# One chunk store of batch 1 split into eight transfers of 6 partitions and one of 80, in an attention and token-update kernel

## The chip, the core and the metric

The kernel runs on one core of one Trainium2 chip. Its work is done by five engines with an instruction stream each: PE (matrix products and transposes), DVE (vector work and copies), ACT (activations and copies), POOL (which issues the loads, gathers and scatters here) and SP (which issues the stores). Transfers run on 16 DMA engines that all queues share. The metric is device time in microseconds (us) of one execution; less is better.

## The reference

For each of 4 batches of 6208 tokens by 256 channels, a channel-by-channel attention is computed, and then 128 chosen tokens of each batch get an update by a small two-layer network:

```python
qn = q / (np.linalg.norm(q, axis=1, keepdims=True) + 1e-06)
kn = k / (np.linalg.norm(k, axis=1, keepdims=True) + 1e-06)
s = kn.transpose(0, 2, 1) @ qn / tau
s = s - s.max(-1, keepdims=True)
a = np.exp(s)
a /= a.sum(-1, keepdims=True) + 1e-09
x = (v @ a).astype(np.float32)
...
scores = np.einsum('bsd,d->bs', x, w_gate)
out = x.copy()
for b in range(B):
    top_idx = np.argpartition(-scores[b], capacity)[:capacity]
    xe = x[b, top_idx]
    h = np.maximum(xe @ w1, 0.0)
    ye = h @ w2
    g = 1.0 / (1.0 + np.exp(-scores[b, top_idx]))
    out[b, top_idx] = x[b, top_idx] + g[:, None] * ye
```

## The kernel before

Each batch is cut into six chunks of 1024 tokens (eight tokens on each of 128 partitions) and a rest of 64 tokens. In the steps below, a batch b goes through these stages.

- **Loads.** POOL issues a load of 1024 tokens of q, of k or of v at L261, cast to bf16 on the way (`qk_ch`, `v_ch`; the rest is `qk_rem`, `v_rem`, L263). First come all q and k of a batch, then its v, then the next batch.
- **Products.** For each q and k chunk PE accumulates the 256 x 256 product and the norms (L426 and L430; for the last batch L411 and L441). When the last chunk is in, the softmax runs on DVE, ACT and PE (L453 to L544) and leaves `a_sb` and the score weights `aw_sb`.
- **v.** PE transposes each half chunk of v (L558), DVE or ACT copies it to `vt_sb` (L576, L579; for the last batch into freed `qk_ch` buffers), PE makes the scores (L607) and the outputs (L641), and ACT or DVE moves the outputs to a `stage` tile (L656, L659). `stage` has 9 buffers of one chunk.
- **Stores.** SP issues the store of a finished chunk: 1 MB, 8 KB from each of 128 partitions (L671), or 64 KB for the rest (L673). Stores of the last batch go as two halves.
- **The update.** Seven rounds of threshold search pick the 128 tokens (L683 to L797: DVE compares at L715, PE counts at L735). POOL then gathers their v rows (`vg`, L803), PE transposes them (L827) and runs the network (L837, L842, L868, L890), DVE makes `upd` (L894), and POOL scatters it over the stored rows (L908), behind the stores of that batch.

Batches are numbered 0 to 3; `L` is 3 and `E` is 2. The stores of batch 2, of batch 3 and of the last two chunks of batch 1 are held back until the last loads have landed: the first of them waits for a piece of the last v chunk, called `GATE`. The outputs of the last two chunks of batch 2 come last and get the update by two more products (L648).

The order of the instructions on every engine is fixed when the kernel is built, by a planner written into it. `Engines` keeps an estimated time for each engine, `Rings` an estimate of the DMA queues; at each step the main loop takes the piece of work that the estimates call ready, by priority. Nothing of this runs on the chip: there the engines run their fixed lists, and wait on semaphores. In `Rings`, `t` is the time up to which the queues are planned, and `lag` holds how far eight of the DMA engines are thought to be behind the others, since PE's instructions are themselves fetched by DMA: each fetch adds `FETCH` to one of the eight in turn, and a transfer is taken to land with the one furthest behind:

```python
self.lag[self.fetched % 8] += FETCH
...
self.lag = [max(0.0, x - (nxt - self.t)) for x in self.lag]
...
self.done[key] = self.t + tail + max(self.lag)
```

When PE would stand idle late in the kernel, the planner puts in products whose result nobody reads (`unread`, L593). Each DMA of SP raises one of eight semaphores in turn (DMAHW0 to DMAHW7 in the lists), and the DMA that takes a semaphore again waits until the transfer that used it last has landed; POOL's loads have eight of their own (DMASW0 to DMASW7).

## Time and profile before

| what | value |
|---|---|
| three timed executions | 258.79, 260.25, 260.44 us (median 260.25) |
| the profiled execution | 259.43 us |
| its span, first to last instruction | 257.4 us |
| PE, DVE, ACT, POOL busy | 206.8, 104.3, 99.4, 56.2 us |
| HBM read and written | 78.91 and 25.95 MB |

The profiled execution took 2.0 us more than its span; the span is what the rows below divide. "Share" of the DMA engines is the mean busy share of all 16, and it can pass 1 a little since a packet's time overlaps the next one's. GB/s counts the bytes on the SBUF side, so a casting load of 1 MB from HBM counts half.

### The profile page before, as it was taken

To read this page: it belongs to the slowest core of one execution; us is meant where nothing else is said; L and a number is where in the kernel's file an instruction comes from. 1 tells how busy PE (TensorE), PEld (TensorE's weight loads), DVE (VectorE), ACT (ScalarE), POOL (GpSimd) and SP (SyncE) were. 2 spreads that over 40 slices of the span, in tenths; PEclk is the share of its full clock that TensorE was granted. 3 is DMA by queue.
4 is the path that set the end of the run, shared out by engine and by line. 5 is a ranking of instruction groups with operands and counts; after the bars stand their busy time and mean duration, and the time that the engine had idled before them with its cause. 6 is when DMAs were issued, how large, how long until landed. Compare 5 with 4: busy or idle time off the path is not lost.

```text
span 257.4 us, 6080 instructions
## 1 busy us (share of the span) xinstructions
PE 206.8 (80%) x2585; PEld 171.4 (67%) x2585; DVE 104.3 (41%) x414; ACT 99.4 (39%) x182; POOL 56.2 (22%) x105
## 2 busy tenths in 40 slices
PE   0099697788888969999998759689998989887980
PEld 0068476676767849997676549577776879665860
DVE  0200002657552263436660011656657266676230
ACT  2800003630000587763943001660233298364750
POOL 8223223123204230100034123213214200001301
PEclk9999889799999997999999799999999999999998
DMA  6999999999999999999999999999999997999995
GB/s 236 259 218 213 213 213 211 215 212 213 213 214 212 214 259 288 279 333 313 315 291 333 308 221 211 214 212 214 211 215 212 212 211 185 402 425 414 401 419 233
DMA packets 16844, 66.84 MB, mean 260 GB/s; under 512 B 2097, under 2 KB 3634, under 8 KB 13618
## 3 DMA queue, kind: packets, MB, share of 16 engines
q0 software_dynamic: 12528, 38.93, 75.8%
q1 hardware_dynamic: 4290, 27.53, 26.4%
q8 instruction: 20, 0.33, 0.5%
q14 instruction: 6, 0.05, 0.0%
HBM read 78.91 MB, written 25.95 MB: 407 GB/s over the span
## 4 chain that ended last, share of the span: by engine, by line
DMA 54%; PE 24%; issue 8%; ACT 4%; DVE 4%; POOL 2%; POOLq 1%; SPq 0%; ACTq 0%
DMA qk_ch<-in_k_dram 29%; DMA qk_ch<-in_q_dram 13%; DMA v_ch<-in_v_dram 12%; PE o_ps L641 8%; PE s_ps L426 4%; PE g_ps L430 4%; ACT stage L659 2%; PE vt_ps L558 2%; PE m_ps L735 1%; PE sc_ps L607 1%; POOL qk_ch L261 1%; ACT vt_sb L576 1%; DVE qk_ch L579 1%; DVE cmp L715 1%; PE g_ps L641 1%
## 5 line engine op out<-in xcount | busy, mean ns | idle before, releaser
L426 PE MATMUL s_ps<-qk_ch 128*128 128x256 bf16 x288 | 68.8, 284 | 21.4 <-DMA qk_ch<-in_k_dram 21.4
L430 PE MATMUL g_ps<-qk_ch 128*128 128x256 bf16 x288 | 68.6, 284 | 0.0
L659 ACT COPY stage<-o_ps 128x512 f32<-128x512 f32 x79 | 44.7, 590 | 40.0 <-PE o_ps L641 38.0
L426 PEld LDWEIGHTS <-qk_ch 128*128 128x128 bf16 x288 | 29.3, 102 | 28.3 <-DMA qk_ch<-in_k_dram 23.3
L641 PE MATMUL o_ps<-a_sb,vt_sb 128*128 128x256 bf16 (+1 forms) x278 | 40.2, 274 | 3.1 <-ACT stage L659 2.1
L641 PEld LDWEIGHTS <-vt_sb 128*128 128x128 bf16 (+1 forms) x294 | 27.5, 98 | 9.9 <-issue 6.0
L430 PEld LDWEIGHTS <-qk_ch 128*128 128x128 bf16 x288 | 29.3, 102 | 4.5
L558 PEld LDWEIGHTS <-v_ch 128*128 128x128 bf16 x384 | 24.5, 101 | 4.2 <-issue 3.5
L558 PE MATMUL vt_ps<-ident_b,v_ch 128*128 128x128 bf16 x328 | 24.9, 226 | 2.9 <-ACT vt_sb L576 2.9
L261 POOL DMA_DIRECT2D qk_ch<-in_q_dram x25 | 13.8, 552 | 44.4 <-PE vt_ps L558 8.7
L261 POOL DMA_DIRECT2D v_ch<-in_v_dram x25 | 13.5, 551 | 29.3 <-DMA qk_ch<-in_q_dram 18.2
L466 DVE SCALAR_TENSOR_TENSOR junk<-g_ps,ident_f 128x128 f32<-128x128 f32 x6 | 1.7, 292 | 44.6 <-ACT e L457 44.5
L261 POOL DMA_DIRECT2D qk_ch<-in_k_dram x25 | 13.6, 545 | 26.7 <-DMA v_ch<-in_v_dram 15.3
L739 DVE TENSOR_REDUCE cnt<-m_ps 128x8 f32<-128x392 f32 (+2 forms) x28 | 12.0, 429 | 16.3 <-PE m_ps L735 15.9
L579 DVE COPY vt_sb<-vt_ps 128x1024 bf16<-128x1024 bf16 x20 | 13.5, 689 | 12.0 <-PE vt_ps L558 12.0
L715 DVE SCALAR_TENSOR_TENSOR cmp<-sc,wl,tab 128x392 bf16<-128x392 f32 x28 | 17.5, 627 | 1.0
L908 POOL DMA_INDIRECT out_dram<-upd,idx x4 | 4.0, 991 | 62.8 <-DMA out_dram<-stage 31.3
L576 ACT COPY vt_sb<-vt_ps 128x1024 bf16<-128x1024 bf16 (+1 forms) x19 | 16.3, 906 | 1.2 <-PE vt_ps L558 1.0
L457 ACT COPY e<-g_ps 128x256 f32<-128x256 f32 x3 | 1.1, 372 | 31.5 <-PE g_ps L430 31.5
L607 PE MATMUL sc_ps<-aw_sb,vt_sb 128*128 128x2 bf16 (+1 forms) x294 | 11.1, 164 | 1.5 <-DVE sc L683 0.6
L441 PE MATMUL s_ps<-qk_ch 128*128 128x256 bf16 x96 | 11.9, 273 | 0.0
L607 PEld LDWEIGHTS <-vt_sb 128*128 128x128 bf16 (+1 forms) x294 | 10.1, 96 | 2.7 <-DVE vt_sb L579 1.6
(180 smaller groups left out, 268.7 us busy)
## 6 DMA issues: line engine op xcount, KB each, us to landing
out_dram<-stage SPq DMA_DIRECT2D x18, 1024.0 KB, 14.3
qk_ch<-in_q_dram POOLq DMA_DIRECT2D x23, 512.0 KB, 14.6
qk_ch<-in_k_dram POOLq DMA_DIRECT2D x23, 512.0 KB, 18.9
v_ch<-in_v_dram POOLq DMA_DIRECT2D x23, 512.0 KB, 16.9
out_dram<-stage SPq DMA_DIRECT2D x12, 512.0 KB, 8.2
stage<-in_moe_w_dram SPq DMA_DIRECT2D x2, 1024.0 KB, 5.0
qk_ch<-in_q_dram POOLq DMA_DIRECT2D x2, 256.0 KB, 16.0
qk_ch<-in_k_dram POOLq DMA_DIRECT2D x2, 256.0 KB
```

The source lines that it names most:

```text
L261: ins = nc.gpsimd.dma_start(out=t[:, rows, :], in_=lview(src, b, d)[:, rows, :])
L426: nc.tensor.matmul(s_ps[:, cc, :].rearrange("p (i c) -> p i c", i=2), lhsT=pair[:parts, 1, s, cc * P:(cc + 1) * P], rhs=pair[:parts, :, s, ...
L430: nc.tensor.matmul(g_ps[:, cc, :].rearrange("p (i c) -> p i c", i=2), lhsT=blocks[:parts, at, :], rhs=blocks[:parts, at:at + step + 1:step ...
L441: nc.tensor.matmul(s_ps[:, cc, :], lhsT=kt[:parts, s, cc * P:(cc + 1) * P], rhs=qt[:parts, s, :], start=d == FIRST and s == 0 and cc == 0, ...
L558: nc.tensor.transpose(vt_ps[:, cc, j, :parts], in_=vt[:parts, v0 + j, cc * P:(cc + 1) * P], identity=ident_b[:parts, :parts])
L576: nc.scalar.copy(vt_sb[:, :, :n, :parts], vt_ps[:, :, :n, :parts])
L579: nc.vector.tensor_copy(vt_sb[:, :, :n, :parts], vt_ps[:, :, :n, :parts])
L607: nc.tensor.matmul(sc_ps[:parts, col, :], lhsT=vt_sb[:, cc, j, :parts], rhs=aw_sb[:, cc, :], start=cc == 0 and col == 0, stop=cc == 1 and ...
L641: nc.tensor.matmul(o_ps[:parts, pj, :], lhsT=vt_sb[:, cc, j, :parts], rhs=a_sb[:, cc, :], start=pj == 0 and cc == 0, stop=last and cc == 1 ...
L659: nc.scalar.copy(st[:parts, rows, :], o_ps[:parts, :m, :])
L715: nc.vector.scalar_tensor_tensor(out=cmp, in0=sc[:, :, None].to_broadcast([P, NCOL, NTHR]), scalar=wl[:, i, NTHR:NTHR + 1], in1=tab[:, Non ...
L739: nc.vector.tensor_reduce(out=cnt9[:, 0:NTHR], in_=mps[:, 0:wide * NTHR].rearrange("p (s j) -> p j s", s=wide), axis=AX.X, op=ALU.add)
```

## The change

The first chunk store of batch 1 is issued in nine DMAs where there was one. Eight of them take 6 partitions each, four partitions apart, out of the first 48 (partitions 0, 4, ..., 20; then 1, 5, ..., 21; and so on, and the same from 24 on); the ninth takes partitions 48 to 127. The planner gets a kind of transfer (`few`) that moves `t` on and takes its duration off all eight entries of `lag`; these may now be below zero and then stay so, and a landing adds no less than zero. As landings are estimated anew, the planner also writes a different order from batch 1 on.

```diff
--- before.py
+++ after.py
@@ -40,8 +40,8 @@
         self.lag[self.fetched % 8] += FETCH
         self.fetched += 1
 
-    def add(self, ring, ready, dur, key, tail):
-        self.q[ring].append((ready, dur, key, tail))
+    def add(self, ring, ready, dur, key, tail, few=False):
+        self.q[ring].append((ready, dur, key, tail, few))
 
     def run(self, until):
         while True:
@@ -51,14 +51,16 @@
             nxt = max(self.t, min(self.q[r][0][0] for r in heads))
             if nxt > until:
                 return
-            self.lag = [max(0.0, x - (nxt - self.t)) for x in self.lag]
+            self.lag = [max(min(0.0, x), x - (nxt - self.t)) for x in self.lag]
             self.t = nxt
             able = [r for r in heads if self.q[r][0][0] <= nxt]
             r = able[0] if len(able) == 1 else 1 - self.last
-            ready, dur, key, tail = self.q[r].pop(0)
+            ready, dur, key, tail, few = self.q[r].pop(0)
             self.last = r
             self.t = nxt + dur
-            self.done[key] = self.t + tail + max(self.lag)
+            if few:
+                self.lag = [x - dur for x in self.lag]
+            self.done[key] = self.t + tail + (0.0 if few else max(0.0, max(self.lag)))
 
     def landing(self, key):
         if key in self.done:
@@ -201,6 +203,8 @@
     LATE = order[-2:]
     BACK = order[-2:]
     LROWS = len(LATE) * RPP
+    UNEVEN = (1, order[0])
+    SIXES = 48
 
     def groups(ci):
         return [(ci, 0, 4), (ci, 4, 4)] if ci < NFULL else [(ci, 0, 1)]
@@ -998,11 +1002,26 @@
         if late(b, ci):
             dep = max(dep, rings.landing(("scatter", E)))
         parts = (2 if b == L else 1) if ci < NFULL else 1
+        uneven = (b, ci) == UNEVEN
+        if uneven:
+            st = stage_of[(b, ci)]
+            for i, p0 in enumerate(range(0, SIXES, 24)):
+                for j in range(4):
+                    ps = slice(p0 + j, p0 + j + 21, 4)
+                    nc.sync.dma_start(out=view(out, b, ci)[ps], in_=st[ps])
+                    issued = eng.issue("sp", 0.75, dep)
+                    key = ("st", b, ci, i, j)
+                    rings.add(1, issued + 0.65, 0.32, key, 0.45, True)
+                    stored[b].append(key)
         for h in range(parts):
             key = ("st", b, ci) if h == parts - 1 else ("st", b, ci, h)
             issued = eng.issue("sp", 0.42, dep)
-            rings.add(1, issued + 0.65, STORE / parts + 0.009 if ci < NFULL else 0.2, key, 0.45)
-            ins = emit_store(b, ci, h, parts)
+            share = (P - SIXES) / P if uneven else 1.0
+            rings.add(1, issued + 0.65, STORE * share / parts + 0.009 if ci < NFULL else 0.2, key, 0.45)
+            if uneven:
+                ins = nc.sync.dma_start(out=view(out, b, ci)[SIXES:P], in_=st[SIXES:P])
+            else:
+                ins = emit_store(b, ci, h, parts)
         stored[b].append(key)
         if not late(b, ci):
             held[b] -= 1
```

On SP, at the stores around the change: before, chunks 4 and 5 of batch 0, chunk 0 of batch 1, its rest, and its chunks 1 to 3 (`128x2048` is a chunk, `64x256` the rest; in brackets what a DMA waits for).

```order
L671 DMA out_dram<-stage 128x2048 [waits DMAHW0_49,Activation_49]
L671 DMA out_dram<-stage 128x2048 [waits DMAHW1_49,Activation_49]
L671 DMA out_dram<-stage 128x2048 [waits DMAHW2_49,Activation_49]
L673 DMA out_dram<-stage_rem 64x256 [waits DMAHW3_49,Activation_49]
L671 DMA out_dram<-stage 128x2048 [waits DMAHW4_49,Activation_49]
L671 DMA out_dram<-stage 128x2048 [waits DMAHW5_49,Activation_49]
L671 DMA out_dram<-stage 128x2048 [waits DMAHW6_49,Activation_49]
```

The same place now, from chunk 5 of batch 0 to chunk 1 of batch 1:

```order
L675 DMA out_dram<-stage 128x2048 [waits DMAHW1_49,Activation_49]
L1011 DMA out_dram<-stage 6x2048 [waits DMAHW2_49,Activation_49]
L1011 DMA out_dram<-stage 6x2048 [waits DMAHW3_49]
L1011 DMA out_dram<-stage 6x2048 [waits DMAHW4_49]
L1011 DMA out_dram<-stage 6x2048 [waits DMAHW5_49]
L1011 DMA out_dram<-stage 6x2048 [waits DMAHW6_49]
L1011 DMA out_dram<-stage 6x2048 [waits DMAHW7_49]
L1011 DMA out_dram<-stage 6x2048 [waits DMAHW0_49]
L1011 DMA out_dram<-stage 6x2048 [waits DMAHW1_49]
L1022 DMA out_dram<-stage 80x2048 [waits DMAHW2_49]
L677 DMA out_dram<-stage_rem 64x256 [waits DMAHW3_49,Activation_49]
L675 DMA out_dram<-stage 128x2048 [waits DMAHW4_49,Activation_49]
```

The short transfers go once round the eight semaphores, so the seventh and the eighth of them now wait for the landing of chunks 4 and 5 of batch 0, and the rest and chunks 1 to 3 of batch 1 stand behind them.

On PE, where the gathered rows (`vg`) of batch 1 are transposed: before, this stands between products of batch 2's q and k.

```order
L430 LDWEIGHTS qk_ch
L430 MATMUL g_ps<-qk_ch 128x256
L827 LDWEIGHTS vg [waits DMASW0_49]
L827 MATMUL vt_ps<-ident_b,vg 128x128
...
L426 LDWEIGHTS qk_ch [waits DMASW7_49]
L426 MATMUL s_ps<-qk_ch 128x256 [waits DMASW6_49]
```

Now it stands behind all of those products, behind the softmax of batch 2 and behind its first transposes of v:

```order
L562 LDWEIGHTS v_ch
L562 MATMUL vt_ps<-ident_b,v_ch 128x128
L831 LDWEIGHTS vg [waits DMASW2_49]
L831 MATMUL vt_ps<-ident_b,vg 128x128 [waits Activation_49]
...
L611 LDWEIGHTS vt_sb
L611 MATMUL sc_ps<-aw_sb,vt_sb 128x2 [waits DVE_49]
```

The whole update of batch 1 has moved with it by some 200 instructions of PE's list. That list has 18 unread products less than before (36 rows of 5136).

On PE near the end, where the gathered rows of batch 3 are transposed: before, behind the last output products (L641, L648).

```order
L648 LDWEIGHTS late_oh
L648 MATMUL o_ps<-d_b,late_oh 128x256
L827 LDWEIGHTS vg [waits DMASW4_49]
L827 MATMUL vt_ps<-ident_b,vg 128x128
...
L593 LDWEIGHTS ident_b
L593 MATMUL sc_ps<-w_sb,ident_b 128x256
L837 LDWEIGHTS a_sb
L837 MATMUL m_ps<-vgt,a_sb 128x128 [waits DVE_49]
```

Now two output tokens' worth of products, eight in all, stand between this transpose and the products that need its copy:

```order
L831 LDWEIGHTS vg [waits DMASW4_49]
L831 MATMUL vt_ps<-ident_b,vg 128x128
...
L645 LDWEIGHTS vt_sb
L645 MATMUL o_ps<-a_sb,vt_sb 128x256 [waits Activation_49]
...
L841 LDWEIGHTS a_sb
L841 MATMUL m_ps<-vgt,a_sb 128x128 [waits DVE_49]
```

So the transpose is issued eight products earlier, and the unread product that stood in the gap is gone.

## Rows read from the trace of the kernel before

**Rows 1.** The profile's page: DMA busy tenths in 40 slices; the chain's shares by engine.

```profile
DMA  6999999999999999999999999999999997999995
...
DMA 54%; PE 24%; issue 8%; ACT 4%; DVE 4%; POOL 2%; POOLq 1%; SPq 0%; ACTq 0%
```

**Rows 2.** Stretches: length, busy of each engine, clock, DMA share, GB/s.

```profile
core 0: us, PE busy (x) PEld busy (x) DVE busy (x) ACT busy (x) POOL busy (x), PEclk, DMA share, GB/s
...
140.00:145.00 5.00, 2.00 (x13) 1.28 (x11) 0.00 (x0) 0.00 (x0) 0.86 (x2) 0.79 1.03 328
...
200.00:210.00 10.00, 9.09 (x149) 7.58 (x142) 3.80 (x21) 4.90 (x11) 1.58 (x3) 1.00 1.09 213
```

**Rows 3.** The same view in short stretches, where the loads end.

```profile
214.00:214.50 0.50, 0.50 (x19) 0.48 (x17) 0.00 (x0) 0.50 (x3) 0.00 (x0) 1.00 0.81 164
214.50:216.00 1.50, 1.34 (x26) 1.04 (x23) 0.32 (x2) 1.08 (x4) 0.00 (x0) 1.00 0.59 108
216.00:216.50 0.50, 0.50 (x16) 0.50 (x14) 0.30 (x1) 0.00 (x0) 0.00 (x0) 1.00 0.35 62
216.50:217.00 0.50, 0.50 (x13) 0.50 (x11) 0.50 (x2) 0.16 (x1) 0.00 (x0) 1.00 0.06 12
```

**Rows 4.** The page's DMA queues: packets, MB, share of 16 engines.

```profile
q8 instruction: 20, 0.33, 0.5%
```

**Rows 5.** The same view as Rows 2, in the stretch of the held stores.

```profile
218.00:222.00 4.00, 3.40 (x76) 2.94 (x74) 2.36 (x5) 0.77 (x1) 0.00 (x0) 1.00 1.01 389
222.00:226.00 4.00, 3.93 (x41) 2.85 (x38) 3.02 (x14) 2.97 (x6) 0.00 (x0) 1.00 1.01 424
...
222.00:248.00 26.00, 23.27 (x247) 18.63 (x244) 12.92 (x53) 16.78 (x31) 2.98 (x3) 1.00 1.02 414
...
252.00:253.00 1.00, 0.00 (x0) 0.00 (x0) 0.00 (x0) 0.00 (x0) 0.83 (x1) 1.00 1.08 459
...
255.00:256.00 1.00, 0.00 (x0) 0.00 (x0) 0.00 (x0) 0.00 (x0) 0.00 (x0) 0.75 0.08 33
```

**Rows 6.** SP: its wait for the gate (us, times, longest), and the first held store.

```profile
SPq L671 <- DMA v_ch<-in_v_dram: 87.5, 1, 87.5
...
216.69 0.33 SPq L671 DMA_DIRECT2D out_dram<-stage  x1
```

**Rows 7.** The end, timeline of DVE and POOL: start us, us, what, and idle before it.

```profile
251.06 0.48 DVE L894 SCALAR_TENSOR_TENSOR upd<-o_ps,gate,xe 128x256 f32<-128x256 f32 x1 [0.45 <-PE o_ps L890]
...
251.86 0.97 POOL L908 DMA_INDIRECT out_dram<-upd,idx  x1 [7.91 <-DVE upd L894]
```

**Rows 8.** SP's timeline around the changed store; last, the page's median time to landing.

```profile
110.68 3.37 SPq L671 DMA_DIRECT2D out_dram<-stage  x2
...
120.03 0.33 SPq L671 DMA_DIRECT2D out_dram<-stage  x1
120.45 0.48 SPq L673 DMA_DIRECT2D out_dram<-stage_rem  x1
123.71 5.41 SPq L671 DMA_DIRECT2D out_dram<-stage  x3
...
out_dram<-stage SPq DMA_DIRECT2D x18, 1024.0 KB, 14.3
```

**Rows 9.** Timeline of POOL, then of PE, in batch 2's first part.

```profile
110.70 0.53 POOL L261 DMA_DIRECT2D qk_ch<-in_k_dram  x1 [2.76 <-DMA qk_ch<-in_k_dram]
131.00 1.01 POOL L908 DMA_INDIRECT out_dram<-upd,idx  x1 [19.77 <-DVE cnt L739]
...
143.48 0.39 PE L426 MATMUL s_ps<-qk_ch 128*128 128x256 bf16 x1 [3.00 <-DMA qk_ch<-in_k_dram]
151.55 0.29 PE L827 MATMUL vt_ps<-ident_b,vg 128*128 128x128 bf16 x2 [3.06 <-DMA vg<-in_v_dram,idx]
```

**Rows 10.** PE's timeline: unread products, the last transpose of v, batch 3's gathered rows.

```profile
210.86 1.04 PE L593 MATMUL sc_ps<-w_sb,ident_b 128*128 128x256 bf16 x8
...
220.36 0.61 PE L558 MATMUL vt_ps<-ident_b,v_ch 128*128 128x128 bf16 x8
...
247.00 0.28 PE L827 MATMUL vt_ps<-ident_b,vg 128*128 128x128 bf16 x2
```

## The prediction

> **What bounds the kernel now.** I read the page's slices first. The 16 DMA engines show 9 tenths or more in all slices but the first, one near 215 us and the last, and the chain that ended last is DMA for 54% [rows 1]. Then I asked each stage what ends last there. Where loads run alone the DMA share is 1.09 at 213 GB/s [rows 2]; that is all 16 engines at work. From 222 to 248 us, where the held stores run, it is 1.02 at 414 GB/s, still 1.08 at 252, and 0.08 only at 255 [rows 5]. So the kernel is a queue of transfers with one hole in it: SP sits on the gate for 87.5 us and issues the first held store at 216.69, when the first piece of the last v chunk has landed [rows 6].
>
> The hole is what this change is about. At 214 us the share begins to fall: 0.81, then 0.59 for 1.5 us, 0.35, 0.06 [rows 3]. Against 1.09, a share of 0.59 is 0.54 of 16, some 8.7 engines. So about seven engines have done all their loads by 214.2 us, and about nine go on to some 216.3, the last to 216.6. A transfer has landed when its slowest engine has, so the whole tail waits for those nine. They lag by 2.3 us. The work left after 214.0 is 0.5 x 0.81 + 1.5 x 0.59 + 0.5 x 0.35 + 0.5 x 0.06 = 1.50 us of share; spread evenly at 1.09 it ends at 214.0 + 1.37 = 215.4. Perfect balance is therefore worth 1.2 us at most.
>
> A cause fits in size: 20 instruction fetches took 0.5% of 16 engines' span [rows 4], 0.005 x 16 x 257.4 / 20 = 1.0 us each. 17 or so of them before the gate, on eight engines alone, make 2.1 us each. No view of this trace names the engine of a packet, so that it is eight fixed ones is inferred.
>
> **The change, part by part.** *The split store.* Held stores move 424 GB/s [rows 5], so 1 MB (1.049 million bytes) takes 2.47 us, and one of the eight rows of 8 KB that each engine then has takes 0.309 us. The changed store gives 80 partitions evenly, 5 rows an engine, and 48 in sixes. The trace holds no transfer of 6 partitions. Its bounds are six engines with one row each time, 8 rows extra, or fewer engines, for instance three with 16 extra; I take six, since the planner's 0.32 us per transfer is nearest to the one row of 0.309. Six engines then carry 13 rows where they had 8, +1.55 us; the other ten carry 5, -0.93 us. If the six are among the seven that are early, they finish at 214.2 + 1.55 = 215.75, and the laggards at 216.6 - 0.93 = 215.7. Both meet: the gate comes 0.9 us earlier. The store stands at 120 us [rows 8], and the DMA share never falls from there to 214 [rows 1], so nothing evens the offset out on the way.
>
> The rule that settles which engines is one of the Trainium skill, DMA: Bandwidth & Descriptors, section "Why a DMA increments its semaphore by 16 and not by 1": a transfer from SP uses the largest number of engines up to 16 that divides its slowest dimension, and the lowest-numbered ones. By that a transfer of 6 partitions runs on engines 0 to 5 and one of 80 on all 16; no run here shows it.
>
> *SP's queue.* Nine DMAs of some 0.3 to 0.5 us [rows 8] in place of one are not the price. The seventh and eighth short ones wait for the semaphores of the chunks issued at 110.68 and by 114.05, and a store takes 14.3 us to land [rows 8]: they go at about 125 and 128, the 80 partitions behind them at 128.5, and the rest and chunks 1 to 3 of batch 1 follow in a row. Before, these went at 120.45, 123.71 and up to 129.1 [rows 8], so chunk 1 comes some 6 us later and chunk 3 about 2. Who waits for that? POOL's scatter of batch 1 stands behind the held stores, 100 us on; `stage` has nine buffers, and chunk 1's is needed again in batch 2. What hides it is the load queue: POOL issued a load at 110.70 and no more until 131.00, and PE still waited for a k load at 143.48 [rows 9], with the DMA share at 1.03 between 140 and 145 [rows 2]. So loads fill the engines while stores are late, and the same bytes end at the same time. If that cover were gone, the engines would idle some 2 to 6 us. I put it at nothing.
>
> *The order.* The update of batch 1 moves behind batch 2's softmax. PE's wait of 3.06 us for its gather [rows 9] goes from that place; late there next are the q and k loads themselves, which PE then meets without that delay. 18 unread products go, at 1.04 / 8 = 0.13 us each [rows 10] 2.3 us of PE. PE needs some of that: the last transpose of v stands at 220.36 [rows 10], 3.8 us after the last load, so PE and the copies, not the load, hold the selection there, and an earlier gate alone would not move it. With up to 5 us of PE time released and loads that land 0.9 earlier, I take PE to follow by at least 0.9; that is the softest step.
>
> *The end.* The last scatter goes at 251.86, released by `upd`, which ends at 251.54 [rows 7], while the DMA engines work through stores until after 253 [rows 5]. Both chains start from the gate or from PE and come 0.9 earlier. The gathered rows of batch 3 are now transposed eight products (8 x 0.11 = 0.9 us) earlier than 247.00 [rows 10]; that can give the update up to 0.5 us, or nothing if the gather has just landed by then. More than that is not to be had, since the stores must drain.
>
> **Sum.** Gate -0.9; SP 0; order 0 beyond keeping pace; end 0 to -0.5, taken as 0. The profiled execution took 259.43, 2.0 more than its span: 259.43 - 0.9 = 258.5. The median of the three runs is 260.25, and the four executions together average 259.7; I forecast 259.7 - 0.9 = 258.8.
>
> **The rivals.** *A, slower: the short transfers cost more than their bytes.* Six engines have no slack left after +1.55, so what each transfer costs beyond 0.309 us goes into the gate eight times; from 0.9 / 8 = 0.11 us each the gain is gone. The nearest row is the stretch 218 to 222, which has a store of 64 KB among its chunks and moves 389 GB/s in place of 424: 4 x 35 / 424 = 0.33 us lost at most to it [rows 5]. Eight times 0.33 is 2.6, the gate comes 1.7 later, 261.4. Fewer than six engines is the same mechanism: three have 21 rows, 13 x 0.309 = 4.0 more, end at 218.2, and give 261.3; two have 29, 6.5 more, end at 220.7, and give 263.8. Against it: the share in that stretch is 1.01, so the engines did not stand still.
>
> Here the Trainium skill speaks against the change: the same page, Rules for kernel authors, has many small transfers put into one, as under 64 KB one pays mostly overhead; its anatomy of one DMA gives some 2 us fixed for each on POOL's path. If the engines were held for all of it, eight would be 16 us, an estimate from that page, and the kernel near 274. The rows above bound what an engine is held at 0.33.
>
> *B, no gain: the six are the laggards, or a mix.* Then the nine end at 216.6 + 1.55, and the time is 259.7 + 1.5 = 261.2; with a mix it lies between that and no change. The trace speaks neither way on which engines lag.
>
> *C, PE does not follow.* The gate moves, but selection and update keep their times, and the scatter goes at 251.86 as before: 259.7. If the products of q and k that now stand among batch 1's threshold rounds wait for loads, it is 1 to 2 us worse, 261.
>
> *D, more.* PE runs free by 3 us and the update's chain was the last thing: 256.9 at best, as stores still drain until 252.
>
> **How the numbers follow.** The forecast has 0.52 (its own range 257.8 to 259.8), C 0.18, A 0.10, B 0.10, D 0.10. About 1%, 2.6 us, is what a measurement of this kernel can tell from no change. Faster by over 1% needs D's far end: 0.06. Slower by over 1% needs A with two engines, or a dearer transfer, or C gone wrong by 3 us: 0.07. The rest, 0.87, lies within 1%. The range reaches from D's 256.9 to B's and A's 261.4, and leaves out A's far end.
>
> **What would show it.** In the changed trace, the share after the loads' end should fall from 1.09 to near nothing within about 1 us instead of 2.5, and the first held store should be issued near 215.8. SP should show waits of some 5 and 3 us among the short transfers, and the DMA share should stay at 1.03 or more between 120 and 150. PE should have no wait of 3 us for the gather of batch 1, and the last transpose of v should come by 219.5. I am wrong if the share still falls in two steps, or if the gate comes earlier and the last scatter does not.

## The result and the profile after

The changed kernel took 262.88 us (median of four runs, 262.22 to 263.55) where the kernel before took 259.93 beside it (258.79 to 260.44). The ratio is 1.011, with a 95% interval from 1.0076 to 1.0144: some 3 us slower, and outside the range of the forecast. In this and all later ratios, runs over 1.5% above their kernel's fastest are left out: one of f1 and four of g1 (the profiled one among them in both), one of g3, one of f2, and one of the kernel before beside the experiments (683.74 us). The profiled execution took 263.55 us, the longest of the four, with a span of 262.0, 4.6 more than the span before.

The page of the changed kernel first: the granted clock and the DMA busy tenths in 40 slices, and the chain that ended last.

```profile
PEclk9999999977999999999997699669999997999999
DMA  7999999999999999999999999999999997599995
...
PE 46%; DMA 27%; ACT 9%; DVE 7%; issue 7%; POOL 1%; POOLq 1%; ACTq 0%; DVEq 0%
```

Two things differ from [rows 1]. Near the loads' end stands a 7 as before, but a 5 follows it: the held stores run, and then stop once more. And the chain has turned round: DMA was 54% of it and PE 24%; now PE is 46% and DMA 27%. Next the stretches that answer to [rows 2, 3, 5] (columns as there).

```profile
140.00:145.00 5.00, 2.26 (x11) 1.65 (x12) 0.00 (x0) 0.00 (x0) 1.44 (x3) 0.64 1.05 324
...
165.00:175.00 10.00, 9.04 (x87) 7.06 (x87) 4.42 (x19) 5.64 (x13) 2.13 (x4) 0.52 1.07 212
...
214.00:215.00 1.00, 1.00 (x17) 0.94 (x15) 0.49 (x2) 1.00 (x3) 0.00 (x0) 1.00 1.14 215
215.00:216.00 1.00, 1.00 (x12) 0.90 (x11) 0.51 (x3) 1.00 (x5) 0.00 (x0) 1.00 0.84 154
216.00:217.00 1.00, 0.52 (x9) 0.34 (x7) 0.90 (x6) 1.00 (x2) 0.00 (x0) 1.00 0.21 39
217.00:218.00 1.00, 0.60 (x12) 0.48 (x13) 0.97 (x5) 1.00 (x3) 0.00 (x0) 1.00 0.15 29
...
226.00:230.00 4.00, 3.90 (x59) 3.07 (x58) 2.49 (x9) 1.66 (x3) 0.00 (x0) 1.00 0.21 84
```

The loads end in two steps again, and the second is now long and thin: 0.21, then 0.15 of the engines, two or three of 16, where nine of them ended [rows 3]. From 226 to 230 us, in the middle of the held stores, the share is 0.21, where [rows 5] have 1.02 from 222 to 248 us. From 165 to 175 us PE's granted clock is 0.52, that is 1.2 GHz for nearly all of it. SP's timeline, around the changed store and at the gate (answers to [rows 6, 8]):

```profile
118.81 7.97 SPq L1011 DMA_DIRECT2D out_dram<-stage  x8
126.83 0.44 SPq L1022 DMA_DIRECT2D out_dram<-stage  x1
127.38 0.52 SPq L677 DMA_DIRECT2D out_dram<-stage_rem  x1
...
217.39 0.33 SPq L675 DMA_DIRECT2D out_dram<-stage  x1
```

The gate opens at 217.39, 0.7 later than before and not 0.9 earlier. PE's timeline shows where it waited and what ran behind the waits:

```profile
142.74 0.40 PE L430 MATMUL s_ps<-qk_ch 128*128 128x256 bf16 x1 [4.56 <-DMA qk_ch<-in_k_dram]
...
152.99 0.28 PE L430 MATMUL s_ps<-qk_ch 128*128 128x256 bf16 x1 [1.67 <-DMA qk_ch<-in_k_dram]
...
157.90 0.28 PE L430 MATMUL s_ps<-qk_ch 128*128 128x256 bf16 x1 [1.25 <-DMA qk_ch<-in_k_dram]
...
165.78 1.19 PE L517 MATMUL m_ps<-diag,ones_f 128*128 128x256 f32 x2 [3.10 <-DVE diag L505]
...
172.04 1.86 PE L872 MATMUL o_ps<-xet,w_sb 128*128 128x128 bf16 x16
```

The 3-us wait for batch 1's gather [rows 9] is gone, as the order said. PE now meets three waits for k, where it had one of 3.00, and one of 3.10 inside batch 2's softmax; the update of batch 1 follows (L872: its network) at half clock. From there PE stays late. On DVE the last scores of batch 3 are reduced from 228.39, and the last `upd` [rows 7] comes 5.6 later than before:

```profile
228.39 0.15 DVE L688 TENSOR_REDUCE sc<-sc_ps 64x1 f32<-64x2 f32 x1 [0.44 <-PE sc_ps L611]
...
256.70 0.48 DVE L898 SCALAR_TENSOR_TENSOR upd<-o_ps,gate,xe 128x256 f32<-128x256 f32 x1 [0.45 <-PE o_ps L894]
```

The first of these rows stood at 222.15 in the kernel before (DVE's timeline):

```profile
222.15 0.15 DVE L684 TENSOR_REDUCE sc<-sc_ps 64x1 f32<-64x2 f32 x1 [0.44 <-PE sc_ps L607]
```

The hole from 226 to 230 us is PE's lateness too. Among SP's waits from 218 to 232 us the longest, which ends at 228.7, is for the copy of an output chunk that isn't made yet:

```profile
SPq L675 <- ACT stage L663: 8.3, 1, 8.3
```

### The profile page after: what moved, and what is told of

It reads as the page before. It is cut to its first block, busy times and chain, and to the rows that moved or that the text cites. A ratio compares the mean times of both kernels' runs of the same rounds, so it can differ in the third digit from the quotient of the medians.

```text
span 262.0 us, 6054 instructions
## 1 busy us (share of the span) xinstructions
PE 212.5 (81%) x2567; PEld 173.7 (66%) x2567; DVE 106.7 (41%) x417; ACT 96.3 (37%) x179; POOL 56.4 (22%) x105
## 4 chain that ended last, share of the span: by engine, by line
PE 46%; DMA 27%; ACT 9%; DVE 7%; issue 7%; POOL 1%; POOLq 1%; ACTq 0%; DVEq 0%
DMA qk_ch<-in_k_dram 27%; PE o_ps L645 8%; PE s_ps L430 6%; PE g_ps L434 6%; PE vt_ps L562 5%; PE sc_ps L611 4%; PE s_ps L445 4%; ACT stage L663 4%; PE g_ps L415 3%; ACT vt_sb L580 3%; PE m_ps L739 2%; PE o_ps L894 2%; PE o_ps L872 1%; ACT e L526 1%; POOL qk_ch L265 1%
## 5 line engine op out<-in xcount | busy, mean ns | idle before, releaser
L430 PE MATMUL s_ps<-qk_ch 128*128 128x256 bf16 x288 | 71.2, 291 | 25.2 <-DMA qk_ch<-in_k_dram 25.2
L434 PE MATMUL g_ps<-qk_ch 128*128 128x256 bf16 x288 | 71.0, 290 | 0.0
L663 ACT COPY stage<-o_ps 128x512 f32<-128x512 f32 x78 | 43.9, 593 | 51.8 <-PE o_ps L645 50.1
L430 PEld LDWEIGHTS <-qk_ch 128*128 128x128 bf16 x288 | 30.0, 104 | 33.1 <-DMA qk_ch<-in_k_dram 27.2
L645 PE MATMUL o_ps<-a_sb,vt_sb 128*128 128x256 bf16 (+1 forms) x274 | 38.7, 272 | 2.6 <-ACT stage L663 1.7
L434 PEld LDWEIGHTS <-qk_ch 128*128 128x128 bf16 x288 | 30.0, 104 | 5.3
L562 PE MATMUL vt_ps<-ident_b,v_ch 128*128 128x128 bf16 x344 | 27.8, 232 | 2.5 <-ACT vt_sb L580 2.5
L562 PEld LDWEIGHTS <-v_ch 128*128 128x128 bf16 x384 | 25.9, 104 | 3.9 <-issue 2.4
L265 POOL DMA_DIRECT2D qk_ch<-in_q_dram x25 | 13.7, 550 | 48.1 <-DMA v_ch<-in_v_dram 8.7
L583 DVE COPY vt_sb<-vt_ps 128x1024 bf16<-128x1024 bf16 x22 | 15.0, 690 | 10.7 <-PE vt_ps L562 10.7
L580 ACT COPY vt_sb<-vt_ps 128x1024 bf16<-128x1024 bf16 (+1 forms) x17 | 14.4, 890 | 0.7 <-PE vt_ps L562 0.7
L611 PE MATMUL sc_ps<-aw_sb,vt_sb 128*128 128x2 bf16 (+1 forms) x294 | 11.9, 165 | 1.0 <-DVE sc L687 0.5
L611 PEld LDWEIGHTS <-vt_sb 128*128 128x128 bf16 (+1 forms) x294 | 10.9, 99 | 2.7 <-DVE vt_sb L583 1.2
L445 PE MATMUL s_ps<-qk_ch 128*128 128x256 bf16 x96 | 12.1, 273 | 0.0
```

Source lines behind the costliest of these rows:

```text
L265: ins = nc.gpsimd.dma_start(out=t[:, rows, :], in_=lview(src, b, d)[:, rows, :])
L430: nc.tensor.matmul(s_ps[:, cc, :].rearrange("p (i c) -> p i c", i=2), lhsT=pair[:parts, 1, s, cc * P:(cc + 1) * P], rhs=pair[:parts, :, s, ...
L434: nc.tensor.matmul(g_ps[:, cc, :].rearrange("p (i c) -> p i c", i=2), lhsT=blocks[:parts, at, :], rhs=blocks[:parts, at:at + step + 1:step ...
L445: nc.tensor.matmul(s_ps[:, cc, :], lhsT=kt[:parts, s, cc * P:(cc + 1) * P], rhs=qt[:parts, s, :], start=d == FIRST and s == 0 and cc == 0, ...
L562: nc.tensor.transpose(vt_ps[:, cc, j, :parts], in_=vt[:parts, v0 + j, cc * P:(cc + 1) * P], identity=ident_b[:parts, :parts])
L580: nc.scalar.copy(vt_sb[:, :, :n, :parts], vt_ps[:, :, :n, :parts])
```

## The experiments

The theories that the expectations name: 1, the new order makes PE late; 2, the uneven bytes delay the loads; 3, half of each; 4, short transfers cost more than their bytes; 5, PE's waits cost because the products behind them run at 1.2 GHz; 6, SP's waits push stores into the time when PE waits for loads; 7, batch 1's update stands in the wrong place.

All eighteen runs, with the ratio to the kernel before on the same chip. Letters e to i stand for five sessions, on four chips, so runs of different letters are compared by their ratios.

| run | what it is | median us | ratio, 95% interval |
|---|---|---|---|
| e1_order | changed order, one store of 128 | 261.08 | 1.0050 (1.0021 to 1.0078) |
| e2_split | order of before, changed store | 261.52 | 1.0064 (1.0030 to 1.0099) |
| e3_even | order of before, eight stores of 16 | 260.74 | 1.0026 (0.9991 to 1.0061) |
| e4_four | order of before, eight of 4 and one of 96 | 260.82 | 1.0054 (1.0029 to 1.0079) |
| f1_after_fill | changed kernel, planner may fill from 136 us | 265.70 | 1.0205 (1.0158 to 1.0251) |
| f2_before_fill | kernel before, the same | 259.62 | 0.9984 (0.9966 to 1.0003) |
| f3_split_fill | e2, the same | 259.95 | 1.0004 (0.9984 to 1.0023) |
| f4_last | order of before, split on the fourth store | 260.21 | 1.0015 (0.9994 to 1.0036) |
| g1_after_busy | changed kernel, 81 unread products in its waits | 263.17 | 1.0083 (1.0047 to 1.0119) |
| g2_split_busy | e2, 64 unread products | 260.41 | 1.0026 (1.0005 to 1.0046) |
| g3_order_busy | e1, 81 unread products | 261.96 | 1.0063 (1.0035 to 1.0092) |
| g4_before_busy | kernel before, 44 unread products | 259.57 | 0.9990 (0.9970 to 1.0010) |
| h1_order_calm | e1, half of batch 1's update moved back | 262.31 | 1.0102 (1.0074 to 1.0129) |
| h2_after_calm | changed kernel, the same | 264.40 | 1.0168 (1.0135 to 1.0201) |
| h3_even_busy | e3, 52 unread products | 259.70 | 0.9999 (0.9974 to 1.0024) |
| h4_gate | kernel before, gate one load earlier | 258.52 | 0.9976 (0.9930 to 1.0022) |
| i1_busy_gate | g4 and h4 together | 259.31 | 0.9988 (0.9961 to 1.0016) |
| i2_fill_gate | f2 and h4 together | 259.38 | 0.9982 (0.9952 to 1.0013) |

### Order and store apart (e1, e2)

e1 keeps everything that the planner plans and issues the store whole:

```diff
-                    ps = slice(p0 + j, p0 + j + 21, 4)
-                    nc.sync.dma_start(out=view(out, b, ci)[ps], in_=st[ps])
...
-            if uneven:
-                ins = nc.sync.dma_start(out=view(out, b, ci)[SIXES:P], in_=st[SIXES:P])
-            else:
-                ins = emit_store(b, ci, h, parts)
+            ins = emit_store(b, ci, h, parts)
```

> The planner plans as in the changed kernel, so every engine but SP has its order; but the store itself goes out as one transfer of 128 partitions. Theory 1 (the new order makes PE late, the split does little): within 0.8 us of the changed kernel's 262.9; half clock again after 165 us, batch 3's update 5 us later than the 251.54 of before. Theory 2 (the split delays the loads, the order alone would keep pace): 259.9 give or take 0.8, the first held store by 216.7. Theory 3 (each half of it): about 261.4, with the half clock gone since the k loads come earlier.

e2 is the kernel before, planner included, with only the emitted DMAs changed:

```diff
-            ins = emit_store(b, ci, h, parts)
+            if (b, ci) == (1, order[0]):
+                st = stage_of[(b, ci)]
+                for p0 in (0, 24):
+                    for j in range(4):
+                        ps = slice(p0 + j, p0 + j + 21, 4)
+                        nc.sync.dma_start(out=view(out, b, ci)[ps], in_=st[ps])
+                ins = nc.sync.dma_start(out=view(out, b, ci)[48:P], in_=st[48:P])
+            else:
+                ins = emit_store(b, ci, h, parts)
```

> The order of before on PE, DVE, ACT and POOL, with the store as eight transfers of 6 partitions and one of 80. Theory 1: 259.9 give or take 0.8, the gate at 216.7 to 217.5. Theory 2: the six engines are a mix of early and late ones; the late of them finish up to 1.55 us later than before, so the gate comes at about 218.2 and the time is 261.4 to 262.9; the DMA share after the loads' end falls in three steps. The forecast on record had 258.8 and a gate at 215.8 for this part.

The order alone costs 0.50%, 1.3 us; the store alone 0.64%, 1.7 us; together that is 3.0, and the changed kernel costs 1.1%, 2.9. So within these intervals the two add, as theory 3 says. e1 speaks against each of the other two as the whole cause: its 261.08 lies outside the 262.1 to 263.7 of theory 1 and the 259.1 to 260.7 of theory 2.

### What of the store costs (e3, e4, f4)

e3 gives every engine the same bytes through as many short transfers (`for p0 in range(8): ps = slice(p0, P, 8)`, eight of 16 partitions). e4 takes four partitions at a time (`ps = slice(j, j + 25, 8)`, eight times) and the other 96 at the end. f4 splits batch 1's fourth store, the last ahead of the gate, and issues the 80 partitions first, so that nothing is queued behind the short ones.

> The order of before, with the same store as eight transfers of 16 partitions, one row of 8 KB for each of 16 engines in each: SP's queue is as full as with the uneven split, but the bytes are even. Theories 1 and 2 (short transfers cost only their bytes): 259.9 give or take 0.8, gate at 216.7, the DMA share's fall after the loads as before, 0.59 for about 1.5 us. Theory 4 (short transfers or SP's waits cost more than their bytes, up to 0.33 us each): 261 or more, gate at 218 or later.

> The order of before, with the store as eight transfers of 4 partitions and one of 96: a few engines, four if each partition has its own, then hold 14 rows where the others hold 6, so they get +1.85 us and the others -0.62. If those are all early ones (of the six, two were late ones and these came last): gate 0.6 earlier, near 216.1, time 259.3. If they are a mix like the six: gate 1 us or more later than before, 260.5 to 262. Theory 1 says at most 0.6 us either way from 259.9.

> The order of before; the split is on batch 1's fourth chunk store in place of its first, with the 80 partitions ahead of the eight short ones, so that no store stands behind the short ones until the gate; the bytes are as uneven as in the change. Theory 2 (uneven bytes on a mix of engines): the loads' 2 us more lag stay, gate at 217.5 or later, 261 to 262. Theory 6 (SP's waits among the short ones push three chunk stores into the time when PE waits for k and for the gather): 259.9 give or take 0.8, and PE's wait for the gather is 3 to 5 us and not 9.1.

e3 is not to be told from no change, and its gate opens at 215.78, where theory 4 has 218 or later, so theory 4 falls: eight transfers of 64 KB show no cost beyond their bytes. The stretches where the loads end show what the uneven bytes do. First f4, whose gate opens at 218.25:

```profile
215.00:216.00 1.00, 1.00 (x37) 0.96 (x35) 0.00 (x0) 1.00 (x4) 0.00 (x0) 1.00 0.53 102
216.00:217.00 1.00, 0.84 (x18) 0.58 (x15) 0.00 (x0) 0.99 (x3) 0.00 (x0) 1.00 0.10 16
217.00:218.00 1.00, 1.00 (x21) 0.95 (x20) 0.71 (x3) 0.00 (x0) 0.00 (x0) 1.00 0.08 12
```

Then e4, whose gate opens at 216.71:

```profile
215.00:216.00 1.00, 1.00 (x22) 1.00 (x20) 0.91 (x3) 1.00 (x3) 0.00 (x0) 1.00 0.68 131
216.00:217.00 1.00, 1.00 (x38) 0.96 (x35) 0.00 (x0) 1.00 (x4) 0.00 (x0) 1.00 0.11 20
```

In f4 the share stays at 0.10 and 0.08 for two microseconds: 0.08 x 16 / 1.09 is 1.2 engines. Everything is done but one engine or two, and the gate waits for them. That fits rival B's mix: most of the six were early ones, but one or two of them were late already, and these now end last. No row names an engine, so it is inferred from the share. With sixes the gates of the five profiles e2, f3, f4, g2 and of the changed kernel open at 217.33, 218.11, 218.25, 219.14 and 217.39; without, in before, e1, e3, f2, g3, g4 and h3, at 215.51 to 216.79. (f1, g1, h1 and h2 have a later gate for another reason, below; h4, i1 and i2 moved it; e4 had fours.) In time the unevenness is smaller than in the gate: f4 costs 0.2 us against before, f3 0.3 against f2, e2 0.8 against e3 and g2 0.8 against g4 (medians); of these four only g2's is clear of the intervals. e4's gate lies among those without sixes, so its ratio of 1.0054 comes from elsewhere: like e2 and e3 it had one long wait for batch 1's gather, of 7.91 us.

f4 also answers theory 6. With no store behind the short ones its PE waits 5.32 us for k and 3.29 for the gather, in two pieces, where e2, e3 and e4 wait 9.13, 7.52 and 7.91 in one; its time is within the 259.9 give or take 0.8 that theory 6 has for it, and its gate where theory 2 has it. So the later stores account for the long wait, as far as one profile of each run can show it, and the uneven bytes for the gate.

### Keeping PE busy (f1 to f3, g1 to g4, h3)

e2's profile shows the other part of the store's cost. PE came to batch 1's gather with its k loads done and waited once and long; the transposes and the products behind it took 0.40 and 0.42 us:

```profile
153.50 0.40 PE L827 MATMUL vt_ps<-ident_b,vg 128*128 128x128 bf16 x2 [9.13 <-DMA vg<-in_v_dram,idx]
153.69 0.42 PE L426 MATMUL s_ps<-qk_ch 128*128 128x256 bf16 x1
```

In the kernel before there were two waits of 3 us at this place, and 0.29 us for the same transposes behind the second [rows 9]. To test the clock, unread products were put into the waits. f1 to f3 let the planner do it, which moves other work too (`if (late_phase() or t > 136.0) and r - t > FILL`); in the g runs and h3 they are written in by hand and nothing else moves:

```diff
+    def raw(n):
+        t = scores_of(sc_last[0])
+        for _ in range(n):
+            nc.tensor.matmul(t[:, 256:512], lhsT=ident_b, rhs=w1_sb[:, 0, 0:256], start=not sc_open[0],
+                             stop=not sc_open[0])
...
+        if b == 1:
+            raw(64)
         for cc in range(2):
             nc.tensor.transpose(tp[:, cc, 0, :], in_=vg[:, cc * P:(cc + 1) * P], identity=ident_b)
```

(g2; 52 there in h3; in g4 22 there and 22 ahead of a k chunk; in g1 and g3 38, 12 and 9 ahead of three chunks and 22 in the softmax.)

> The changed kernel, but the planner may put in unread products from 136 us of its own time on, where it did so only after batch 2's softmax; PE's waits for k loads and for the softmax of batch 2 get some 65 of them. Theory 5 (what costs is PE's clock: a wait of 3 to 9 us is followed by products at 1.2 GHz, two stretches of 6.8 and 10.2 us in the changed kernel): the clock stays at 1.00 from 145 to 190, the update ends 3 to 5 us earlier, and the time is 259 to 260.5. If the clock is no cause, the added products cost what they last or nothing: 262.9 to 264.

> The kernel before with the same permission to fill. It has one stretch at half clock only, 142.9 to 146.3 us, so theory 5 gives at most 1 us: 258.7 to 259.6. It separates what filling gives by itself from what it gives back in the changed kernel; a gain of over 2 us here would say that filling helps whatever the order.

> The kernel before with fill, and with the split store (eight of 6 partitions, one of 80). Against the run of before's order with the split store, 261.5, in which PE waited 9.1 us for batch 1's gather and then ran at 1.2 GHz: theory 5 says the 2 us of slow products come back, 259.3 to 260.2, and what is left over the kernel with fill alone is the lag of the late engines, up to 1.5. Theory 2 (lag alone): 261.5 as before the fill.

> The changed kernel in exactly its order on every engine, with 81 unread products put into PE's four waits of batch 2 (38, 12 and 9 ahead of three q and k chunks, 22 ahead of the softmax's transposes); the run that filled by way of the planner had moved the gather of batch 2 too. Theory 5 (what costs is products at 1.2 GHz behind a wait): PE's clock stays at 1.00 from 145 to 190, the threshold rounds of batch 2 begin 3 to 4.5 us earlier than at 185.8, and the time is 259.5 to 261.3; the lag of the split is left. If the clock is only a companion: 262.5 to 264.

> The order of before with the split store, and 64 unread products ahead of batch 1's gathered rows, where PE waited 9.13 us. Theory 5: the products behind it run at 2.4 GHz, some 2 us come back, 259.7 to 260.4 where the same without them took 261.5; PE still waits some 1 to 2 us there. Theory 2 (only the lag costs): 261.5.

> The changed order with one store of 128 partitions, and the same 81 unread products. No lag is added, so theory 5 has no cost left: 258.5 to 260, at or below the kernel before; the threshold rounds of batch 2 begin near 179.5 where they began at 183.8. If the order costs for another reason: 260.5 to 261.5 as without them.

> The kernel before with 22 unread products in each of its two 3-us waits (for k at 143.48, for the gather at 151.55). One stretch of half clock, 142.9 to 146.3 us, is all it has to give back, and most of that lies ahead of the wait for the gather: theory 5 says 259 to 260, no more than 0.5 us below before. A gain of over 1 us would mean that keeping PE busy helps by itself, and the other runs of this kind would have to be read against this one.

> The order of before, the store as eight even transfers of 16 partitions, and 52 unread products ahead of batch 1's gathered rows, where PE waited 7.5 us and then ran at 1.2 GHz. No lag is added here, so it tests the clock alone. Theory 5: the rounds of batch 2 begin near 180.2 (182.2 without the products), the gate stands at 215.9 as without them, so both chains end by 257.0 and the time is 258.9 to 259.4. If the clock is no cause: 260.7 as without.

With the order of before, the runs go the way of theory 5: the ratio falls from 1.0064 in e2 to 1.0026 in g2 and 1.0004 in f3, and from 1.0026 in e3 to 0.9999 in h3. Only f3's step is clear of the intervals, and f3 moved other work too. h3's stretches show the clock held, where e3 had 0.50 from 150 to 155, and its last scores of batch 2 are reduced at 177.56 where e3's are at 179.72 (from 170 to 175 us its clock is 0.66 and e3's 0.82, so the products did not hold it everywhere):

```profile
145.00:150.00 5.00, 5.00 (x48) 4.49 (x46) 0.00 (x0) 0.00 (x0) 0.56 (x2) 1.00 1.06 332
150.00:155.00 5.00, 3.98 (x40) 3.36 (x39) 1.15 (x4) 0.37 (x1) 1.12 (x3) 1.00 1.07 217
```

With the changed order they don't: g3 has 1.0063 where e1 has 1.0050, and g1's 1.0083 against 1.0110 is within the intervals, with a median of 263.17 over its eleven runs. g3's profiled run, at 259.83, is one of its three best. In it the clock is 1.00 from 140 to 190 us. The last scores of batch 2 are reduced (DVE's timeline) in the kernel before, in e1, in g3 and in f3 at:

```profile
176.44 0.24 DVE L686 TENSOR_REDUCE sc<-sc_ps 128x48 f32<-128x96 f32 x1
...
181.39 0.24 DVE L690 TENSOR_REDUCE sc<-sc_ps 128x48 f32<-128x96 f32 x1
...
179.73 0.24 DVE L700 TENSOR_REDUCE sc<-sc_ps 128x48 f32<-128x96 f32 x1
...
179.94 0.24 DVE L686 TENSOR_REDUCE sc<-sc_ps 128x48 f32<-128x96 f32 x1
```

So in g3's profile 1.7 us of e1's 5.0 are gone, with the clock, and 3.3 stayed at full clock. Why g3's other runs took up to 262.7 the profile of a short run can't say.

f3 bears on the 3.3. Between batch 2's softmax and its last scores PE's order is that of before, but for batch 1's update, which the planner put there as the changed order does, and a few output products and products of batch 3 that it moved; its clock is 1.00 from 140 to 190 us. From PE's product with the diagonal in that softmax (166.27) to the last scores it took 13.7 us, where the kernel before, at full clock too, took 10.9 (from 165.58) and g3 15.6 (from 164.13). So some 2.8 us go with the update's place there; its products last 3.2 us.

### Moving the update back, and the gate (h1, h2, h4, i1, i2)

h1 and h2 change one constant of the planner's rule that holds an update back (`> now() + 6.0` to `4.0`). Half of batch 1's update then stands ahead of the last q and k products again.

> The changed order with the single store, but the planner's rule that holds batch 1's update back while v of batch 2 is less than 6 us from landing has 4 us: the first half of the update goes ahead of the last q and k products again, its network behind the softmax. Theory 7 (the order costs because the update of batch 1, some 4 us of PE, moved out of PE's wait for loads into the stretch between the softmax and the scores of batch 2, which passes to the end): the threshold rounds of batch 2 begin by 182.0 where they began at 183.8, and the time is 259.5 to 260.3. Theory 5 (clock alone): 260.8 to 261.5 if half clock follows the softmax again.

> The changed kernel, split store included, with that one constant at 4 in place of 6. Theory 7: the scores of batch 3 come 1.5 to 3 us earlier than 228.2; the end is then the later of two chains, 40.8 us behind the gate (217.4 to 218.2, since the split's lag is left) and 33.7 us behind the last scores: 260.3 to 261.8 in place of 262.9. Theory 5: 262.3 to 263.5.

Both are slower than without, so these two don't confirm theory 7. POOL's timeline of h2 shows what got in the way: the gather of batch 2 waits for the selection, and eight v loads are queued behind it.

```profile
202.90 1.00 POOL L807 DMA_INDIRECT vg<-in_v_dram,idx  x1 [10.91 <-DVE tokl L814]
203.87 0.61 POOL L265 DMA_DIRECT2D v_ch<-in_v_dram  x1
204.41 0.66 POOL L267 DMA_DIRECT2D v_rem<-in_v_dram  x1
204.93 3.38 POOL L265 DMA_DIRECT2D v_ch<-in_v_dram  x6
```

The loads run dry meanwhile:

```profile
200.00:210.00 10.00, 10.00 (x224) 8.41 (x221) 4.95 (x25) 1.28 (x3) 5.41 (x9) 1.00 0.62 99
```

Its gate opens at 221.74, h1's (gather at 199.96, share 0.90) at 219.18. g1 (gather at 205.63) has a share of 0.80 there, and f1 one of 0.32 and a gate at 225.58, but these two profiles are of runs that no ratio counts. In the changed kernel the gather goes at 202.75, but only five loads stand behind it and the share is 1.03.

h4 releases the held stores one load earlier (`load_inst[GATE]` to `load_inst[("v", 0) + units[-2]]`); i1 and i2 add that to g4 and f2.

> The kernel before in its own order, with the held stores released by the v load ahead of the last chunk in place of the last chunk's first half, about 2 us earlier. If the end hung on the gate alone: 2 us faster, 257.6. By the two chains (40.8 us behind the gate, 33.7 behind the last scores, the later of both): the last v chunk then shares the engines with stores and lands 1.5 to 2.5 us later, the scores come at 223.5 to 224.4 and the end at 257.2 to 258.1 after the span's start, so the time is 259.3 to 260.2, no gain.

> The kernel before with both things that the runs pointed to: PE kept busy in its two waits of batch 2 (22 unread products each, all such runs stayed at a mean clock of 0.957 or more), and the held stores released by the load ahead of the last v chunk. By the two chains: the gate comes some 1.3 us earlier (its chain ends near 255.9), the last scores stay at 222.6 (their chain ends at 256.2), so the span is 256.2 and the time 258.0 to 258.6, faster than both kernels. By the gate alone: 257.2 to 257.7. If the earlier stores hold up the last v chunk: 259.5.

> The kernel before with fill by way of the planner (259.6 without the new gate) and the earlier release. There batch 1's update stands behind the softmax, the last scores come at 224.3, and their chain, 33.6 us, sets the end at 257.9: by the two chains the earlier gate brings nothing, 259.4 to 259.9. If the end hung on the gate: 258.2 to 258.6.

Four of h4's six runs took 257.45 to 258.58, and two 261.09 and 261.13, one of which was profiled. In that run PE had one wait of 6.70 us for the gather of batch 1 and the half clock behind it, though its edit touches only the release of the held stores, at 216.57:

```profile
151.57 0.39 PE L827 MATMUL vt_ps<-ident_b,vg 128*128 128x128 bf16 x2 [6.70 <-DMA vg<-in_v_dram,idx]
151.75 0.42 PE L426 MATMUL s_ps<-qk_ch 128*128 128x256 bf16 x1
```

So the long wait is a thing that the order of before meets too, in some runs. i1 and i2 are a hair faster than before and not by more than the measurement can tell; i1's gate opens at 215.40, but its last score came at 223.77 and not at 222.57 as in g4. No version here beats the kernel before by a measurable amount; h4's three shortest runs lie below the shortest of the kernel before (258.47), but six runs are too few to tell.

## Why the prediction was wrong, point by point

**The end is the later of two chains.** Twenty profiles, the two kernels and eighteen experiments, give one relation: the span is the later of 40.8 us behind the first held store and 33.6 us behind the start of the reduction of batch 3's last scores. The two constants were read from the first profiles and stand (as 40.8 and 33.7) in h2's expectation; the six runs from there on agree. It is a fit to these profiles; what fills the 40.8 and the 33.6 was not varied.

| kernel | first held store | +40.8 | last scores | +33.6 | span |
|---|---|---|---|---|---|
| before | 216.69 | **257.5** | 222.15 | 255.8 | 257.4 |
| after | 217.39 | 258.2 | 228.39 | **262.0** | 262.0 |
| e1 | 215.51 | 256.3 | 226.39 | **260.0** | 260.0 |
| e2 | 217.33 | 258.1 | 225.87 | **259.5** | 259.4 |
| e3 | 215.78 | 256.6 | 225.41 | **259.0** | 259.1 |
| f4 | 218.25 | **259.1** | 223.56 | 257.2 | 259.0 |
| g2 | 219.14 | **259.9** | 225.03 | 258.6 | 260.0 |
| g3 | 216.63 | 257.4 | 224.66 | **258.3** | 258.1 |
| h1 | 219.18 | **260.0** | 225.76 | 259.4 | 260.0 |
| h2 | 221.74 | **262.5** | 228.70 | 262.3 | 262.7 |
| h3 | 216.51 | **257.3** | 222.81 | 256.4 | 257.6 |
| h4 | 216.57 | 257.4 | 225.41 | **259.0** | 259.0 |
| i1 | 215.40 | 256.2 | 223.77 | **257.4** | 257.2 |
| i2 | 215.41 | 256.2 | 223.87 | **257.5** | 257.3 |

(All within 0.3; the other six fit within 0.2.) In the kernel before, the gate's chain leads by 1.7 us, so its last scores could come 1.7 us later at no cost. The forecast had both chains, but took them as coming forward together, and never worked out how much later PE could get before its own set the end.

**The gate, -0.9.** Wrong in sign: +0.7 in the changed kernel, and +0.6 to +2.5 over the five profiles with sixes. The step that failed is "if the six are among the seven that are early": it was a condition, and no row bore on it. What the runs show in its place is a tail of one to three engines and a gate that came later. Rival B had this mechanism at 261.2 with a tenth of the chance; e2 measured 261.52, but only about half of that by the gate and the late loads. By the Trainium skill (DMA: Bandwidth & Descriptors, "Why a DMA increments its semaphore by 16 and not by 1") these six are engines 0 to 5 each time. A long thin tail that appears with sixes and not with the even split fits a fixed set, but no view names an engine, so which of them lag stays open.

**SP's queue, 0.** Right for the transfers: the eight short ones took 7.97 us, chunk 1 went at 128.32, 4.6 us later than [rows 8], and the DMA share stayed at 1.03 or more. The term left PE out. Behind the later stores PE waited 7.5 to 9.1 us for the gather at one time (e2, e3, e4) and then ran at half clock, and this was not among the rivals. With PE kept busy (h3) nothing of it is left that the runs can tell.

**The Trainium skill's rule against it** (same page, Rules for kernel authors, small transfers into one). Rival A's further estimate from that page, 16 us, did not appear: eight transfers of 64 KB measured 1.0026 and 0.9999 (e3, h3), and eight of 48 KB 1.0015 (f4). Where page and measurement differ, the measurement decides: with the DMA share at 1.03 and more, as here, no overhead shows.

**The order, "PE to follow by at least 0.9".** This is the step that cost most. The last scores of batch 3 came 6.2 us later, 4.2 of it in e1 by the order alone. The freed wait was real: PE's product with the diagonal in batch 2's softmax stood at 163.88 in e1 and at 165.58 before (with the split store, 165.78, the gain is gone). But what was counted as a gain became the loss. The 18 unread products were nothing to win: 44 more of them cost nothing measurable (g4, 0.9990). The update of batch 1 had run beside the loads, and now stands between the softmax and the scores of batch 2. In e1 these scores ended 5.0 us later; 1.7 of that was gone in the profile with full clock, and 3.3 was not. f3 puts 2.8 on the update's place; that this is what keeps e1 late is argued from f3 and the order, not shown, since h1 and h2, which were to move the update alone, moved the loads too. Nor does the place alone cost much at the end: f2 and f3, with the update there, have their last scores of batch 3 at 224.27 and 224.35, some 2.1 us later than before against the 1.7 us of slack, and f2 measures 0.9984. Why g3's median is no better than e1's stays open.

**The sum of rivals.** B and a worse C came together, and by e1 and e2 they add. The range, built from one rival at a time, ended at 261.4. (D's 256.9 has no working; 259.7 less 3 is 256.7.)

**The tests.** The DMA share at 120 to 150 and the vanished gather wait came out as written; the single-step end of the loads, the gate at 215.8 and the last transpose of v by 219.5 (it came at 226.61) did not. Of SP's forecast waits of 5 and 3 us among the short transfers there was one, of 2.1.

## What to carry to other kernels

Before bytes are shifted between DMA engines, find out with a small uneven transfer which engines it lands on and whether these are the early ones, since the slowest engine alone sets when a load has landed. Write the end as the later of its chains, each with its own slack, before an order is changed: work that stands beside another engine's transfers costs little there, and can cost its full time elsewhere. And rivals that act on different chains or stretches can come true together, so a range should hold their sum.

## What the hardware showed that I had not expected

**The clock differs from run to run.** PE's mean granted clock is not the same in all runs of one kernel, and in the kernel before and in e3 the time goes with it. Of 131 runs of the kernel before made beside the experiments, 23 had a mean granted clock of 0.943 or less and took 259.89 to 261.65 us, median 261.01; the other 108 had a median of 259.58. e3 splits the same way: six runs at 0.947 or less took 261.07 to 261.85, six at 0.952 or more 259.40 to 260.41. All four runs of the changed kernel were at 0.938 to 0.946. With unread products in the two waits, g4's twelve runs stayed at 0.957 or more and within 259.31 to 260.06, and i1's twelve at 0.948 or more: the products bought no speed at the best run, but none of these 24 runs fell to 0.943.

**An offset between DMA engines lasts.** The uneven bytes went out at 119 to 127 us, and in the changed kernel the loads still ended in a thin tail of two or three engines 90 us later (shares of 0.21 and 0.15), with the DMA share at 9 tenths or more in every slice between.
